# Chunked attention with a feed-forward layer: the softmax weights and the turned tokens of the later pairs by way of DRAM

## The chip, the cores and the metric

The kernel runs on one core of a Trainium2 chip. A core has five engines that run on their own and wait for each other by semaphores: TensorE (PE in the profile; its weight loads are PEld), VectorE (DVE), ScalarE (ACT), GpSimd (POOL) and SyncE (SP), which here only issues transfers. The metric is device time in microseconds (us); lower is better. A transfer (DMA) is issued by an engine's queue, here nearly always SyncE's, in program order, and is carried out by 16 DMA engines.

## The reference

Attention within chunks of 64 positions, then a normalised feed-forward layer, all in float32:

```python
scores = scale * np.matmul(q_c, k_c.transpose(0, 1, 2, 4, 3))    # (8, 8, 9, 64, 64)
scores = scores - np.max(scores, axis=-1, keepdims=True)
attn = np.exp(scores)
attn = attn / (np.sum(attn, axis=-1, keepdims=True) + 1e-09)
out = np.matmul(attn, v_c)
...
x = np.ascontiguousarray(attn_out.transpose(0, 2, 1, 3)).reshape(B, S, H * D)    # (8, 576, 512)
...
mu = np.mean(x, axis=-1, keepdims=True)
var = np.mean((x - mu) ** 2, axis=-1, keepdims=True)
xn = (x - mu) / np.sqrt(var + 1e-06) * g_ln
ch = np.maximum(xn @ w_ch1, 0.0) @ w_ch2
return (x + ch).astype(np.float32)
```

The 8 x 576 tokens are 4608 rows of 512 features; the hidden layer has 2048.

## The kernel before

**Pairs, tiles, units.** The 4608 tokens are 18 *pairs* of 256 (two blocks of 128 partitions). Two pairs are a tile, nine tiles in all. The first three tiles (pairs 0 to 5) go through a plain feed-forward (`ffn`, its products at L552 and L576) while the weights are brought in and prepared. The other six tiles are three *units* of four pairs: unit 0 is pairs 6 to 9, unit 1 is 10 to 13, unit 2 is 14 to 17. `unit_ffn` computes a unit: 28 pairs of products with seven prepared combinations of the first weights (L803, 336 products of 128x128 by 128x512), then the second weights (L888, 384 products). Its results between the two are made by ScalarE's copies (L809), VectorE's sums (L812), and the split of the hidden values into two parts (L825 on ScalarE, L830 on VectorE).

**Who runs beside whom.** `weave` interleaves the unit's products with the attention of the *next* unit's pairs: while unit 0 is computed, pairs 10 to 13 are prepared, during unit 1 pairs 14 to 17. The order is written out by hand. `attention` and `combine` are generators; `weave` counts products as it goes, and when the count reaches a position it runs the next step of the generator. Pair n of a unit begins at n * 130 + 8 (`PAIR_SPAN`, `LOADED`), and its steps come at `begin + STEPS[i]`; the loads of the pair behind it are issued with the first of them. `combine` runs 11 steps from position 345 (`FIRST_HALF`) and from 592 (`LAST_HALF`), nine apart. A unit has 720 positions. Each engine takes its instructions strictly in this order, so an instruction that waits holds all that was issued behind it on that engine, SyncE's transfers included.

**The weights' ring.** L803 and L888 read their weights from six places in SBUF that SyncE refills from DRAM (L712), one 512 KB transfer for each 12 products, each issued when the products that used the place are done.

**One pair's attention**, for the pairs at hand (neither `by_pe` nor `den_by_pe`), step by step: loads of q and k (L272); the scores, 64 small products (L300); the row maxima (L307) and the loads of v (L317); the subtraction (L332); the exponential (L335); then the softmax weights, whose rows are queries, have to be turned so that keys lie on the partitions. VectorE's transposition turns blocks of 32x32, so this takes 16 instructions of 32 partitions by 256 in four steps, each with another pair of quarters (L360, into `pt_sb`). Then the row sums and their reciprocals (L367 to L369), the outputs, 64 small products with `pt_sb` as stationary operand (L389), the scaling (L423), the statistics (L433, L434, L438, and L439 on GpSimd) and the spilling of x to DRAM (L256), the centred tokens xg on ScalarE (L452), their transposition in blocks (L478, one instruction of 128x1024, into `turned`), 16 transfers of 32 KB in four steps that put the blocks in their places in `rows` (L486, SBUF to SBUF), and the scaling with g on ScalarE (L492).

The large tiles of this chain, p_sb, pt_sb, xg and turned, share the pool `work`, which has two buffers, so a tile waits until the one that holds its buffer has been read for the last time.

**Combining.** `combine` makes the seven combinations of the turned tokens that L803 multiplies: VectorE subtracts in place (L759), and `part` splits each into a rounded part (a copy on ScalarE, L755) and the rest (a subtraction on GpSimd, L756).

**Ahead of unit 0**, the dictionary `THIRD` holds the order for the third tile's products; in it G is the attention of pair 7, which takes the same path as above, H that of pair 9, which lets TensorE turn the weights and tokens, and P and Q are `combine`.

Of the kernel before, what the change touches and what calls it, by code (L numbers as in the profile page):

```python
# [8 lines left out]
F32 = mybir.dt.float32  # L9
# [5 lines left out]
ALU = mybir.AluOpType  # L15
AX = mybir.AxisListType

P = 128
B, H, S, D = 8, 8, 576, 64
# [3 lines left out]
PAIR = 2 * P  # L23
NPAIR = T // PAIR
NTILE = NPAIR // 2
HP = H // 2
NK = DM // P
# [8 lines left out]
LEAD = 3  # L36
# [7 lines left out]
}  # L44
THIRD = {
    0: "CS", 1: "CS", 2: "DDGS", 3: "DS", 4: "DDS", 5: "DS", 6: "GS", 7: "GGHS", 8: "DG", 9: "D", 10: "GGP",
    11: "GGH", 12: "G", 13: "G", 14: "GGHP", 15: "GP", 16: "GHP", 17: "GGHP", 18: "GGHHP", 19: "HP", 20: "HHP",
    21: "HP", 22: "GPP", 23: "H", 24: "H", 26: "QQ", 27: "QR", 28: "Q", 29: "QXXN", 30: "QQR", 31: "Q",
}
ROOMS = {1: (3, 9), 2: (6,)}  # L50

PAIR_SPAN = 130
LOADED = 8
STEPS = (0, 6, 11, 16, 22, 30, 38, 46, 54, 60, 66, 72, 82, 88, 96, 106, 116, 126, 150)
ONE_STEP = 9
FIRST_HALF = 345
LAST_HALF = 592
# [36 lines left out]
def quad(i):  # L94
    return slice(32 * i, 32 * i + 32)
# [3 lines left out]
def chunk_attention_ffn(ctx: ExitStack, tc: tile.TileContext, qkv, v01, g, w, out):  # L99
    nc = tc.nc  # L100
# [4 lines left out]
    work = ctx.enter_context(tc.tile_pool(name="work", bufs=2))  # L105
    xtp = ctx.enter_context(tc.tile_pool(name="xt", bufs=2))
# [9 lines left out]
    dram = ctx.enter_context(tc.tile_pool(name="dram", bufs=1, space=bass.MemoryType.DRAM))  # L116
# [145 lines left out]

    def attention(pair, xt_cols, xs, by_pe, den_by_pe, rows_of=None, pt_raw=False):

        if pair == 1:
            qk = const.tile([P, 2, HP, PAIR], F32, name="qk_b", tag=f"w{NF - 4}")
            q_t, k_t = qk[:, 0], qk[:, 1]
        else:
            q_t = load.tile([P, HP, PAIR], F32, name="q_t")
            k_t = load.tile([P, HP, PAIR], F32, name="k_t")  # L270
# [5 lines left out]
        groups = 2 * HP  # L276
# [16 lines left out]
        s = [rows(s2[:, h2, :]) for h2 in range(2)]  # L293
        for j in range(2):
            for a in range(HP):
                for h2 in range(2):
                    r = slice(h2 * D, (h2 + 1) * D)
                    for c in range(2):
                        cs = slice(j * P + c * D, j * P + (c + 1) * D)
# [19 lines left out]
            nc.sync.dma_start(g_all, g)  # L319
        yield  # L320
        p_sb = work.tile([P, groups, 2, D], F32, name="p_sb", tag="work")
        p_b = p_sb.rearrange("p a b d -> p b a d")
        top4 = top.rearrange("p b (a one) -> p b a one", one=1).broadcast_to([P, 2, groups, D])
        if den_by_pe:
# [15 lines left out]

        if pt_raw:
            pt_sb = raws.tile([P, groups, 2, D], F32, name="pt_raw", tag="wf")
        else:
            pt_sb = work.tile([P, groups, 2, D], F32, name="pt_sb", tag="work")
        if by_pe:
            pt = halves()
            for a in range(groups):
                cs = slice(a % HP * P, (a % HP + 1) * P)
                nc.tensor.transpose(out=pt[a // HP][:, cs], in_=p_sb[:, a, :, :], identity=ident)
            for j in range(2):  # L350
                nc.scalar.copy(
                    pt_sb[:, j * HP : (j + 1) * HP], pt[j].rearrange("p (a c t) -> p a c t", a=HP, c=2)
                )
            yield
        else:
            for h2 in range(2):
                for j in range(2):
                    for c in range(2):
                        for i in range(2):
                            nc.vector.transpose(  # L360
                                out=pt_sb[quad(2 * h2 + j), :, c, quad(i)], in_=p_sb[quad(2 * c + i), :, h2, quad(j)]
                            )
                    yield
# [8 lines left out]
        if by_pe:  # L372
            o2 = banks()
            o = [o2[:, h2, :] for h2 in range(2)]
        else:
            o = [ps_h.tile([P, DM], F32, name="h") for _ in range(2)]
# [5 lines left out]
        for j in range(2):  # L382
            for a in range(HP):
                for h2 in range(2):
                    r = slice(h2 * D, (h2 + 1) * D)
                    ja = j * HP + a
                    for c in range(2):
                        cs = slice(c * D, (c + 1) * D)
# [12 lines left out]
        x = keep.tile([P, 2, DM], F32, name="x")  # L401
        if den_by_pe:
# [3 lines left out]
                out=x_j[:, 0], in0=o4[:, :, :, :D], in1=r_b[:, :, :HP].broadcast_to([P, 2, HP, D]), op=ALU.mult  # L406
            )
            for h2 in range(2):
                nc.vector.tensor_tensor(
                    out=x_j[:, 1, h2], in0=o_j[1][h2][:, :, :D], in1=r_b[:, h2, HP:].broadcast_to([P, HP, D]),  # L410
                    op=ALU.mult,
                )
            taken.remove(pair)
        elif by_pe:
            nc.vector.tensor_tensor(
                out=x.rearrange("p j (a b d) -> p b (j a) d", a=HP, b=2),
                in0=o2.rearrange("p b (a d) -> p b a d", d=D),
                in1=rden.rearrange("p a (b one) -> p b a one", one=1).broadcast_to([P, 2, groups, D]), op=ALU.mult,
            )
# [24 lines left out]
        if rows_of:  # L444
            if not by_pe:
                turned = work.tile([P, 4, 2 * NK, 32], F32, name="turned", tag="work")
            centre = small.tile([P, 2], F32, name="centre")
            nc.vector.scalar_tensor_tensor(
                out=centre, in0=mv[:, :, 0], scalar=-1.0, in1=rstd, op0=ALU.mult, op1=ALU.mult
# [5 lines left out]
        else:  # L455
            for j in range(2):
                nc.vector.scalar_tensor_tensor(
                    out=xg[:, j, :], in0=x[:, j, :], scalar=mv[:, j, 0:1], in1=g_sb, op0=ALU.subtract, op1=ALU.mult
# [1 line left out]
        yield  # L460

        if rows_of and by_pe:
            rows_t = rows_of().rearrange("p j i (k t) -> p j k i t", k=NK)
            xt = halves()
            for j in range(2):
                for k in range(NK):
                    ks = slice(k * P, (k + 1) * P)
                    nc.tensor.transpose(out=xt[j][:, ks], in_=xg[:, j, ks], identity=ident)
                for k in range(NK):
                    nc.scalar.activation(  # L470
                        rows_t[:, j, k], xt[j][:, k * P : (k + 1) * P].rearrange("p (i t) -> p i t", i=4), AF.Copy,
                        scale=g_cols[:, k : k + 1],
                    )
                yield
            return

        if rows_of:
            nc.vector.transpose(  # L478
                out=turned.rearrange("p b a t -> p a b t"),
                in_=xg.rearrange("p j (k b f) -> p (j k) b f", k=NK, b=4),  # L480
            )
            yield
            rows_t = rows_of()
            for i in range(4):
                for b in range(4):
                    nc.sync.dma_start(  # L486
                        rows_t[quad(b), :, i], turned[quad(i), b].rearrange("p (j k) t -> p j (k t)", j=2)
                    )
                yield
            for k in range(NK):  # L490
                x = rows_t.rearrange("p j i (k t) -> p (j i) k t", k=NK)[:, :, k]
                nc.scalar.activation(x, x, AF.Copy, scale=g_cols[:, k : k + 1])  # L492
            yield
            return

        xth, xtl = xt_cols()
        if by_pe:
            xt = halves()
# [21 lines left out]
        else:  # L520
            xt = work.tile([P, 2 * NK, P], F32, name="xt", tag="work")
# [214 lines left out]
    shared = {}  # L736

    def rows_of(i):
        if "rows" not in shared:
            shared["rows"] = [xtp.tile([P, 2, 2, NK, P], F32, name="rows", tag=f"xt{c}") for c in "hl"]  # L740
        return shared["rows"][i // 2][:, i % 2]

    def operand(name):
        if name not in shared:
            shared[name] = const.tile([P, 2, 2, 2 * PAIR], F32R, name="xc", tag=f"w{'2165734'.index(name)}")
        return shared[name]

    def combine(half):
        cs = slice(half * PAIR, (half + 1) * PAIR)
        a, b = (r[:, half].rearrange("p j i (k t) -> p k (j i) t", k=NK) for r in shared["rows"])  # L750
        b11, b21, b12, b22 = a[:, :2], a[:, 2:], b[:, :2], b[:, 2:]

        def part(name, x):
            o = operand(name)[:, :, :, cs].rearrange("p h k (j t) -> p h k j t", t=32)
            nc.scalar.copy(o[:, 0], x)  # L755
            nc.gpsimd.tensor_tensor(out=o[:, 1], in0=x, in1=o[:, 0].bitcast(F32), op=ALU.subtract)  # L756

        def less(out, x, y):
            nc.vector.tensor_tensor(out=out, in0=x, in1=y, op=ALU.subtract)  # L759

        part("2", b21)
        yield
        part("1", b11)
        yield
        less(b11, b12, b11)
        yield
        less(b12, b22, b12)
        yield
# [12 lines left out]
        part("4", b21)  # L781
        yield
# [205 lines left out]
    with tc.manual_schedule():  # L988
# [4 lines left out]
            G=tiles[3].attention(1), H=tiles[4].attention(1, True, pt_raw=True), S=prepare(), R=start_ring(), P=combine(0), Q=combine(1),  # L993
# [61 lines left out]
```

## Time and profile before

| | |
|---|---|
| median of 3 runs | 851.72 us (850.63 to 852.61) |
| profiled execution | 852.83 us |
| its span, first to last instruction | 851.1 us |
| TensorE's clock, mean granted | 0.999 |
| ScalarE busy | 290.0 us |
| VectorE busy | 498.1 us |
| GpSimd busy | 149.4 us |
| DMA engines, mean share by SyncE's transfers | 65.5% |

The span is what the profile covers; the execution's time lies 1.7 us above it. "Idle before, releaser" in a group's row is the time that the engine stood still just before these instructions, with what ended it. PE's idle time is what counts where TensorE is the bound; the idle time of another engine costs nothing by itself. SPq stands for SyncE's queue.

### The profile page before, as it was taken

The page shows a single profiled execution, that of the slowest core. Times are in us where ns is not written, and L with a number is a line of the kernel's source. Part 1 is how long each engine was busy: PE and PEld are TensorE (multiplying, and loading weights), DVE is VectorE, ACT ScalarE, POOL GpSimd, SP SyncE. Part 2 cuts the span into 40 slices and gives each one's busy share as a digit, 9 for nine tenths or more (in the row PEclk, how much of TensorE's full clock was granted, in tenths as well). Part 3 has the DMA queues.
Part 4 walks back from the last instruction along what each step waited for, and adds up shares of the span by engine and source line. Part 5 has one row for each costly group of instructions (what it writes and reads, how often), then busy time and mean ns, then how long its engine had stood idle before and what let it go on. Part 6 is the DMA issues. An engine that isn't in the chain of part 4 may idle for free.

```text
span 851.1 us, 14767 instructions
## 1 busy us (share of the span) xinstructions
PE 833.6 (98%) x5850; PEld 682.8 (80%) x5850; DVE 498.1 (59%) x810; ACT 290.0 (34%) x479; POOL 149.4 (18%) x138
## 2 busy tenths in 40 slices
PE   7999999999999999999999999999999999999998
PEld 4888888888888878888778888887778888888886
DVE  6989956787446536585886627658785221232321
ACT  5766431123422343234342503324534112232220
POOL 0111006474731133000220400000312200000000
PEclk9999999999999999999999999999999999999999
DMA  9997407948981237687676969777587776667572
GB/s 355 336 282 203 174 24 271 319 152 277 329 289 59 68 147 290 194 280 226 252 257 235 359 192 318 230 255 280 166 288 274 255 239 191 196 195 245 189 276 105
DMA packets 80565, 197.34 MB, mean 232 GB/s; under 512 B 8944, under 2 KB 32496, under 8 KB 78576
## 3 DMA queue, kind: packets, MB, share of 16 engines
q1 hardware_dynamic: 79200, 191.68, 65.5%
q0 software_dynamic: 1296, 4.72, 2.9%
q8 instruction: 46, 0.75, 0.4%
q14 instruction: 23, 0.19, 0.1%
HBM read 147.08 MB, written 39.85 MB: 220 GB/s over the span
## 4 chain that ended last, share of the span: by engine, by line
PE 79%; DVE 11%; DMA 3%; SPq 3%; ACT 2%; issue 1%; POOL 0%; DVEq 0%; ACTq 0%; POOLq 0%
PE y L803 22%; PE y L888 18%; PE y L576 13%; PE h L552 13%; PE h L888 8%; DVE pt_sb L360 4%; SPq L486 3%; PE s L300 2%; PE h L389 1%; DMA wp<-wfs 1%; DMA rows<-turned 1%; DMA k_t<-qkv 1%; DVE stats L433 1%; DVE hu L812 1%; PE s L389 0%
## 5 line engine op out<-in xcount | busy, mean ns | idle before, releaser
L803 PE MATMUL y<-xc,ring 128*128 128x512 f32 x1008 | 232.6, 391 | 0.0
L803 PEld LDWEIGHTS y<-xc,ring 128*128 128x128 f32 x1008 | 188.3, 188 | 39.5
L552 PE MATMUL h<-xth,wp 128*128 128x512 f32 (+1 forms) x432 | 129.5, 370 | 1.1 <-DMA wp<-wfs 1.1
L888 PE MATMUL y<-ring,hx 128*128 128x512 f32 x486 | 127.5, 390 | 1.1 <-ACT hx L825 0.8
L888 PEld LDWEIGHTS y<-ring,hx 128*128 128x128 f32 x486 | 90.9, 188 | 21.6 <-ACT hx L825 1.6
L812 DVE TENSOR_TENSOR hu<-y,snap 128x512 f32<-128x512 f32 x72 | 48.5, 683 | 91.9 <-ACT snap L809 48.0
L576 PE MATMUL y<-wp,hh 128*128 128x512 f32 x376 | 96.2, 394 | 0.0
L552 PEld LDWEIGHTS h<-xth,wp 128*128 128x128 f32 x432 | 78.2, 188 | 15.7 <-DMA wp<-wfs 1.3
L360 DVE STREAM_TRANSPOSE pt_sb<-p_sb 32x256 f32<-32x256 f32 x176 | 76.7, 436 | 11.9 <-DMA rows<-turned 6.9
L756 POOL TENSOR_TENSOR xc<-rows,xc 128x512 fp32r<-128x512 f32 x42 | 58.9, 1413 | 126.5 <-ACT xc L755 76.2
L576 PEld LDWEIGHTS y<-wp,hh 128*128 128x128 f32 x376 | 69.1, 188 | 13.9
L809 ACT COPY snap<-y 128x512 f32<-128x512 f32 x72 | 41.8, 586 | 110.0 <-PE y L803 106.7
L552 PE MATMUL h<-xtl,wp 128*128 128x512 f32 (+1 forms) x216 | 78.2, 367 | 0.0
L566 DVE SCALAR_TENSOR_TENSOR hl<-h,hh 128x512 fp32r<-128x512 f32 (+1 forms) x53 | 33.0, 629 | 72.7 <-ACT hh L565 72.4
L888 PE MATMUL y<-ring,hh 128*128 128x512 f32 x252 | 70.0, 391 | 0.0
L565 ACT ACTIVATE hh<-h 128x512 fp32r<-128x512 f32 (+1 forms) x53 | 28.5, 545 | 103.7 <-PE h L552 103.7
L830 DVE SCALAR_TENSOR_TENSOR hx<-hu,hx 128x512 fp32r<-128x512 f32 x54 | 42.8, 797 | 34.2 <-PE h L888 19.7
L888 PEld LDWEIGHTS y<-ring,hh 128*128 128x128 f32 x252 | 46.9, 188 | 10.0
L830 DVE SCALAR_TENSOR_TENSOR hl<-hu,hh 128x512 fp32r<-128x512 f32 x42 | 30.8, 737 | 39.1 <-PE h L888 16.7
L576 PE MATMUL y<-wp,hl 128*128 128x512 f32 x188 | 51.8, 389 | 0.0
L825 ACT ACTIVATE hx<-hu 128x512 fp32r<-128x512 f32 x54 | 33.3, 627 | 53.7 <-PE y L888 30.5
L888 PE MATMUL h<-ring,hx 128*128 128x512 f32 x162 | 49.9, 389 | 0.0
(132 smaller groups left out, 954.3 us busy)
## 6 DMA issues: line engine op xcount, KB each, us to landing
ring<-w2d SPq DMA_DIRECT2D x96, 512.0 KB, 4.6
ring<-wa SPq DMA_DIRECT2D x84, 512.0 KB, 4.4
raw<-w SPq DMA_DIRECT2D x15, 1024.0 KB, 7.2
out<-x SPq DMA_DIRECT2D x36, 256.0 KB, 4.7
q_t<-qkv SPq DMA_DIRECT2D x17, 512.0 KB, 5.4
k_t<-qkv SPq DMA_DIRECT2D x17, 512.0 KB, 6.5
v_t<-qkv SPq DMA_DIRECT2D x32, 256.0 KB, 6.0
w2d<-wp SPq DMA_DIRECT2D x16, 512.0 KB, 6.9
```

The costliest lines, as they stand in the source:

```text
L360: nc.vector.transpose(out=pt_sb[quad(2 * h2 + j), :, c, quad(i)], in_=p_sb[quad(2 * c + i), :, h2, quad(j)])
L552: nc.tensor.matmul(h, lhsT=(wh, wh, wl)[m][:, ks], rhs=(xth, xtl, xth)[m][:, k, :], start=i == 0, stop=i == len(terms) - 1,)
L565: nc.scalar.activation(hh, h, AF.Relu)
L566: nc.vector.scalar_tensor_tensor(out=hl, in0=h, scalar=0.0, in1=hh.bitcast(F32), op0=ALU.max, op1=ALU.subtract)
L576: nc.tensor.matmul(sums(pairs[j // 2])[j % 2], lhsT=(hh, hh, hl)[m], rhs=(wh, wl, wh)[m], start=f == 0 and m == 0, stop=f == NF - 1 and m ...
L756: nc.gpsimd.tensor_tensor(out=o[:, 1], in0=x, in1=o[:, 0].bitcast(F32), op=ALU.subtract)
L803: nc.tensor.matmul(bank, lhsT=w[:, (0, 0, 1)[m], ks], rhs=x[:, (0, 1, 0)[m], k, :], start=start and k == m == 0, stop=k == 1 and m == 2, s ...
L809: nc.scalar.copy(out, bank)
L812: nc.vector.tensor_tensor(out=out, in0=bank, in1=s, op=ALU.add)
L825: nc.scalar.activation(hh, x, AF.Relu)
L830: nc.vector.scalar_tensor_tensor(out=hl, in0=x, scalar=0.0, in1=hh.bitcast(F32), op0=ALU.max, op1=ALU.subtract)
L888: nc.tensor.matmul(ys[j], lhsT=(hh, hh, hl)[m], rhs=w[:, (0, 1, 0)[m]], start=f == 0 and m == 0, stop=f == NF - 1 and m == 2,)
```

## The change

For pairs 10 to 17 (`moved`), one transposition of the whole 128x1024 block of exponentials replaces the 16; the blocks are then put in their places by DRAM: one transfer out, and four in, one for each quarter of 32 partitions. The tile that comes back, `pt_m`, has the queries eight words apart, so the outputs' stationary operand is read with that step. For pairs 7 and 10 to 17, the turned tokens go the same way in place of the 16 transfers within SBUF. `rows` gets another layout for this, in which `part` has to be done in two halves. The steps and their positions are written anew: 16 instead of 19, and the outputs stand at 86 instead of 60. In `THIRD` pair 7 has two steps fewer, and two of pair 9's come one token later.

```diff
-    11: "GGH", 12: "G", 13: "G", 14: "GGHP", 15: "GP", 16: "GHP", 17: "GGHP", 18: "GGHHP", 19: "HP", 20: "HHP",
-    21: "HP", 22: "GPP", 23: "H", 24: "H", 26: "QQ", 27: "QR", 28: "Q", 29: "QXXN", 30: "QQR", 31: "Q",
+    11: "GGH", 12: "G", 13: "G", 14: "GGHP", 15: "GP", 16: "GHP", 17: "GHP", 18: "GHHP", 19: "HP", 20: "HHP",
+    21: "HP", 22: "GPP", 24: "H", 25: "H", 26: "QQ", 27: "QR", 28: "Q", 29: "QXXN", 30: "QQR", 31: "Q",
...
-STEPS = (0, 6, 11, 16, 22, 30, 38, 46, 54, 60, 66, 72, 82, 88, 96, 106, 116, 126, 150)
+STEPS = (0, 6, 11, 16, 22, 28, 44, 56, 86, 91, 97, 107, 113, 119, 135, 174)
...
+        moved = rows_of and not by_pe and pair >= 2 * LEAD + 4
...
+        if moved:
+            p_t = work.tile([P, 4, 32, groups], F32, name="p_t", tag="work")
...
+        if moved:
+            nc.vector.transpose(
+                out=p_t.rearrange("p b q a -> p a b q"), in_=p_sb.rearrange("p a h (j k) -> p a (h j) k", j=2)
+            )
+            yield
+            pt_there = dram.tile([P, 4, 32 * groups], F32, name="pt_there", tag=f"pt_there{pair}")
+            nc.sync.dma_start(pt_there, p_t.rearrange("p b q a -> p b (q a)"))
+            yield
+            pt_m = work.tile([P, 4, 32 * groups], F32, name="pt_m", tag="work")
+            for b in range(4):
+                nc.sync.dma_start(pt_m[quad(b)], pt_there[:, b].rearrange("(s k) x -> k s x", s=4))
+            yield
+            pt_sb = pt_m.rearrange("p (c i) (q a) -> p a c (i q)", c=2, a=groups)
...
+            there = dram.tile([P, 4, PAIR], F32, name="there", tag=f"there{pair}")
+            nc.sync.dma_start(there, turned.rearrange("p b a t -> p b (a t)"))
+            yield
             rows_t = rows_of()
-            for i in range(4):
-                for b in range(4):
-                    nc.sync.dma_start(
-                        rows_t[quad(b), :, i], turned[quad(i), b].rearrange("p (j k) t -> p j (k t)", j=2)
-                    )
-                yield
+            for b in range(4):
+                nc.sync.dma_start(rows_t[quad(b)], there[:, b].rearrange("(i f) x -> f i x", i=4))
+            yield
...
         def part(name, x):
-            o = operand(name)[:, :, :, cs].rearrange("p h k (j t) -> p h k j t", t=32)
-            nc.scalar.copy(o[:, 0], x)
-            nc.gpsimd.tensor_tensor(out=o[:, 1], in0=x, in1=o[:, 0].bitcast(F32), op=ALU.subtract)
+            for j in range(2):
+                o = operand(name)[:, :, :, cs].rearrange("p h k (j i t) -> p h j k i t", j=2, t=32)[:, :, j]
+                y = x[:, :, j::2]
+                nc.scalar.copy(o[:, 0], y)
+                nc.gpsimd.tensor_tensor(out=o[:, 1], in0=y, in1=o[:, 0].bitcast(F32), op=ALU.subtract)
```

More of the change, by code (lines that the diff above doesn't have):

```diff
@@ L342, in attention @@
             pt_sb = raws.tile([P, groups, 2, D], F32, name="pt_raw", tag="wf")
-        else:
+        elif not moved:
             pt_sb = work.tile([P, groups, 2, D], F32, name="pt_sb", tag="work")
-        if by_pe:
+        if moved:
[11 more added lines that the diff above has]
+            pt_sb = pt_m.rearrange("p (c i) (q a) -> p a c (i q)", c=2, a=groups)
+        elif by_pe:
             pt = halves()
@@ L462, in attention @@
         if rows_of and by_pe:
-            rows_t = rows_of().rearrange("p j i (k t) -> p j k i t", k=NK)
+            rows_t = rows_of().rearrange("p i (j k t) -> p j k i t", j=2, k=NK)
             xt = halves()
@@ L482, in attention @@
             yield
+            there = dram.tile([P, 4, PAIR], F32, name="there", tag=f"there{pair}")
+            nc.sync.dma_start(there, turned.rearrange("p b a t -> p b (a t)"))
+            yield
             rows_t = rows_of()
[L484 to L489 removed]
+            for b in range(4):
+                nc.sync.dma_start(rows_t[quad(b)], there[:, b].rearrange("(i f) x -> f i x", i=4))
+            yield
             for k in range(NK):
[L491 removed]
+                x = rows_t.rearrange("p i (j k t) -> p (i j) k t", j=2, k=NK)[:, :, k]
                 nc.scalar.activation(x, x, AF.Copy, scale=g_cols[:, k : k + 1])
@@ L739, in rows_of @@
         if "rows" not in shared:
-            shared["rows"] = [xtp.tile([P, 2, 2, NK, P], F32, name="rows", tag=f"xt{c}") for c in "hl"]
+            shared["rows"] = [xtp.tile([P, 2, 4, PAIR], F32, name="rows", tag=f"xt{c}") for c in "hl"]
         return shared["rows"][i // 2][:, i % 2]
@@ L749, in combine @@
         cs = slice(half * PAIR, (half + 1) * PAIR)
-        a, b = (r[:, half].rearrange("p j i (k t) -> p k (j i) t", k=NK) for r in shared["rows"])
+        a, b = (r[:, half].rearrange("p i (j k t) -> p k (i j) t", j=2, k=NK) for r in shared["rows"])
         b11, b21, b12, b22 = a[:, :2], a[:, 2:], b[:, :2], b[:, 2:]
         def part(name, x):
-            o = operand(name)[:, :, :, cs].rearrange("p h k (j t) -> p h k j t", t=32)
-            nc.scalar.copy(o[:, 0], x)
-            nc.gpsimd.tensor_tensor(out=o[:, 1], in0=x, in1=o[:, 0].bitcast(F32), op=ALU.subtract)
+            for j in range(2):
[3 more added lines that the diff above has]
+                nc.gpsimd.tensor_tensor(out=o[:, 1], in0=y, in1=o[:, 0].bitcast(F32), op=ALU.subtract)
         def less(out, x, y):
```

## The prediction

> **What bounds the kernel now.** I read the chain of work that ended last first, then the busy time by stage, then TensorE's timeline and its waits in the two stages that the change reaches. The chain's shares by line:
>
> ```profile
> PE y L803 22%; PE y L888 18%; PE y L576 13%; PE h L552 13%; PE h L888 8%; DVE pt_sb L360 4%; SPq L486 3%; PE s L300 2%; PE h L389 1%; DMA wp<-wfs 1%; DMA rows<-turned 1%; DMA k_t<-qkv 1%; DVE stats L433 1%; DVE hu L812 1%; PE s L389 0%
> ```
>
> TensorE's products fill the chain, yet two things that the change rewrites stand on the chain: the weights' transpositions (L360, 4%) and SyncE issuing the turned tokens' transfers (L486, 3%). How much of that is lost time follows from the stages. Below are unit 0, unit 1 and unit 2 (stretch, its length, then PE busy and its instructions first):
>
> ```profile
> 327.50:506.10 178.60, 175.64 (x1233) 143.25 (x1233) 115.34 (x193) 60.52 (x107) 24.61 (x19) 1.00 0.73 251
> 506.10:683.65 177.55, 175.53 (x1233) 143.21 (x1233) 114.18 (x192) 60.00 (x106) 23.71 (x18) 1.00 0.75 255
> 683.65:851.10 167.45, 163.20 (x720) 134.79 (x719) 44.25 (x65) 38.52 (x64) 0.00 (x0) 0.99 0.64 207
> ```
>
> Unit 2 has no attention beside it: 720 products in 163.20 us, 0.2267 us each, the pace at full clock (1.00, 0.99). Units 0 and 1 have the same 720 and eight groups of 64 small products (four pairs, scores and outputs). TensorE's timeline (start, length) prices one group, and shows the worst stall:
>
> ```profile
> 345.06 1.16 PE L389 MATMUL h<-v_t,pt_sb 64*64 64x64 f32 x64
> 346.15 15.26 PE L803 MATMUL y<-xc,ring 128*128 128x512 f32 x66
> 361.34 1.16 PE L300 MATMUL s<-k_t,q_t 64*64 64x64 f32 x64
> ...
> 443.77 0.33 PE L389 MATMUL h<-v_t,pt_sb 64*64 64x64 f32 x4
> 444.96 0.30 PE L389 MATMUL h<-v_t,pt_sb 64*64 64x64 f32 x2 [0.86 <-DVE pt_sb L360]
> 445.79 1.14 PE L389 MATMUL h<-v_t,pt_sb 64*64 64x64 f32 x58 [0.54 <-DVE pt_sb L360]
> 446.86 1.20 PE L888 MATMUL y<-ring,hh 128*128 128x512 f32 x4
> ```
>
> From 345.06 to 361.34 are 16.28 us; 66 products take 14.96, so an undisturbed group costs 1.32. The group at 443.77 holds TensorE for 3.09 instead of 1.09. A unit without stalls would take 163.20 + 8 x 1.32 = 173.76 us: unit 0 loses 4.84, unit 1 loses 3.79, together **8.63 us**. That is all that the change can win in them. TensorE's waits there, unit 0, then unit 1 (total, times, longest):
>
> ```profile
> PE h L389 <- DVE pt_sb L360: 2.3, 4, 0.9
> PE y L888 <- ACT hx L825: 0.4, 1, 0.4
> PE y L888 <- DVE hx L830: 0.3, 1, 0.3
> ```
> ```profile
> PE h L389 <- DVE pt_sb L360: 1.6, 3, 0.7
> PE y L888 <- ACT hx L825: 0.4, 1, 0.4
> ```
>
> Idle is 3.9 us at the output groups and 1.1 at L888; the 8.63 (idle, and each restart of the pipeline) I divide likewise: **6.7 us at L389**, 1.9 at L888. Why L389 waits shows on VectorE and on SyncE's queue ahead of the stall at 443.77:
>
> ```profile
> 436.82 3.58 DVE L360 STREAM_TRANSPOSE pt_sb<-p_sb 32x256 f32<-32x256 f32 x8 [2.54 <-DMA rows<-turned]
> 440.43 0.95 DVE L830 SCALAR_TENSOR_TENSOR hx<-hu,hx 128x512 fp32r<-128x512 f32 x1
> 441.42 1.79 DVE L360 STREAM_TRANSPOSE pt_sb<-p_sb 32x256 f32<-32x256 f32 x4
> 443.22 0.69 DVE L830 SCALAR_TENSOR_TENSOR hl<-hu,hh 128x512 fp32r<-128x512 f32 x1
> 443.92 1.81 DVE L360 STREAM_TRANSPOSE pt_sb<-p_sb 32x256 f32<-32x256 f32 x4
> ```
> ```profile
> 432.48 2.50 SPq L486 DMA_DIRECT2D rows<-turned  x4
> 435.08 0.53 SPq L712 DMA_DIRECT2D ring<-w2d  x1
> 435.71 0.38 SPq L272 DMA_DIRECT2D q_t<-qkv  x1
> ```
>
> The pool `work` has two buffers; pt_sb's is the one that the previous pair's `turned` leaves, so VectorE stands 2.54 us until the last of 16 small transfers has landed, then needs 7.2 us for 16 transpositions, and the outputs stand behind them.
>
> **The change, part by part.**
>
> ```profile
> L360 DVE STREAM_TRANSPOSE pt_sb<-p_sb 32x256 f32<-32x256 f32 x176 | 76.7, 436 | 11.9 <-DMA rows<-turned 6.9 <-ACT p_sb L335 2.4
> ...
> L478 DVE STREAM_TRANSPOSE turned<-xg 128x1024 f32<-128x1024 f32 x9 | 11.2, 1244 | 10.6 <-ACT xg L452 10.6
> ```
>
> *Transpositions.* 16 x 0.436 = 7.0 us become one of 128x1024, as L478: 1.24. The new one writes with a step of 32 bytes, which no row shows; bounds 1.24 and twice that, 2.5. I take 1.24, and the other 1.2 would only come off the slack worked out below, since the outputs stand 64 positions behind it. VectorE loses 8 x 5.8 = 46 us of work in the two units and, when `turned` leaves by one transfer, the wait for its buffer (6.9 in all). What L389 waited for on VectorE is gone: **-6.7 us**.
>
> *The trip through DRAM.* What is late next is this. Count from the start T of a pair's scores; positions are products of 0.2267 us.
>
> ```profile
> 394.73 1.16 PE L300 MATMUL s<-k_t,q_t 64*64 64x64 f32 x64
> ```
> ```profile
> 400.11 1.06 ACT L335 ACTIVATE p_sb<-p_sb 128x1024 f32<-128x1024 f32 x1 [0.60 <-DVE p_sb L332]
> ```
>
> The exponentials end at T + 6.4, the transposition at T + 7.7; SyncE comes to position 28 at 1.32 + 6.35 = T + 7.7. The nearest rows for the transfers are the spilled tokens (512 KB out to DRAM), the values (256 KB in) and L486 on SyncE (issue, then size and landing):
>
> ```profile
> DMA to landing us min/median/max: 2.7/3.4/6.5
> ```
> ```profile
> DMA to landing us min/median/max: 3.0/6.0/13.2
> ```
> ```profile
> L486 SPq DMA_DIRECT2D rows<-turned x144: 585/594/1669, 282.2 to 643.7; - x144
> ```
> ```profile
> rows<-turned SPq DMA_DIRECT2D x144, 32.0 KB, 2.2
> ```
>
> Out: landed at T + 11.1 (14.2 at worst); SyncE stands at position 44, T + 11.3, by then. Four transfers in at 0.59 each: issued by T + 13.7, landed by T + 15.9 if they land as L486's do (2.2), by T + 19.7 at the values' 6.0. The outputs stand at 1.32 + 86 x 0.2267 = **T + 20.8**. Slack is 1.1 to 4.9 us at medians, and at the worst of all rows (14.2 + 2.4 + 13.2 = 29.8) the outputs are 9.0 late. I take nothing, near the medians. While SyncE waits, the ring's fetches stand behind it, for up to 3 us here; six places, each used for 12 products (2.7 us), leave a fetch five uses, 13.6 us, to land, so nobody waits for that.
>
> *The outputs' weight loads.* They now read every eighth word.
>
> ```profile
> L389 PEld LDWEIGHTS h<-v_t,pt_sb x704: 129/135/135, 151.1 to 624.2; 64*64 64x64 f32 x176
> L389 PE MATMUL h<-v_t,pt_sb x704: 218/218/267, 151.1 to 624.3; 64*64 64x64 f32 x176
> ```
>
> All these loads read neighbouring words; no row has a load with a step. Below nothing is excluded, the count stays. At the other end, a load at half pace: the group's 1.16 us less the last product's 0.22 is 0.94 of starts, in which loads and products run side by side; doubled, each pair's outputs cost 0.94 more, 8 x 0.94 = 7.5 us. I take nothing, by the nearest row, and keep 7.5 for the range.
>
> *The turned tokens.* 16 issues of 0.59 become five. From the transfers in (position 135) to the scaling (174) are 39 positions, 8.8 us, against 2.4 + 6.0 at the values' median: hidden by products. If it isn't, ScalarE stands at the scaling with L809's copies behind it; `combine` only follows at 345, when the first two pairs have been done since 312. For pair 7, ahead of unit 0, I count nothing: bounds are 1 us either way, about TensorE's one wait there.
>
> *The split of `part`.* 14 copies and 14 subtractions per call of `combine` for 7 and 7, half as wide.
>
> ```profile
> L756 POOL TENSOR_TENSOR xc<-rows,xc 128x512 fp32r<-128x512 f32 x42 | 58.9, 1413 | 126.5 <-ACT xc L755 76.2 <-DMA ring<-w2d 38.6 <-PE y L888 7.6
> ...
> L492 ACT ACTIVATE rows<-rows,g_sb 128x256 f32<-128x256 f32 x36 | 15.3, 497 | 19.3 <-DMA rows<-turned 19.3
> ```
>
> A half-wide copy is 0.50 at most by L492, so a part is at most 1.0 on ScalarE; on GpSimd between 1.41 and 2.8 for two. A part has nine positions, 2.0 us, and GpSimd is idle beside it. But L888 waits for ScalarE, which gets more work: I leave all 1.9 us of L888's stalls.
>
> **The sum.** -6.7 + 0. The profiled execution took 852.83 (span 851.1, 1.7 around it): 846.1. It is 1.1 above the median of the runs, 851.72, so the median comes to **845.0**, 0.8% faster.
>
> **The rivals.**
>
> *1, the loads pay for their step (same time).* For it: loads and products of a group fill the 0.94 us side by side with nothing to hide a slower load. Against: nothing but the missing row. 846.1 + 7.5, as a median 852.5.
>
> [...]
>
> *2, the trip is late (slower).* In the fourth pair of a unit, the brought-back tokens and the next pair's loads share the transfers, and they are full:
>
> ```profile
> 444.00:446.00 2.00, 0.61 (x18) 0.40 (x18) 1.91 (x5) 0.00 (x0) 0.00 (x0) 1.00 1.03 422
> ```
>
> (share 1.03 of 16 engines, 422 GB/s). Half of the 9.0 us of lateness in that pair of both units is 9.0: 855.1, as a median 854.0. It ends slower than before once the eight pairs are late by 6.7 us together. Against: without the 16 issues SyncE, which now issues the next pair's loads (435.71) only after the last of the 16, can send them ahead of the trip.
>
> *3, loads at a third of the pace:* 15 us, a median of 860.
>
> *4, the change does not do what it says:* VectorE's L812 and L830, not the transpositions, hold the outputs, and the stall moves with them: half is won, 848.4.
>
> **Chances.** Forecast 0.50 (its own range 842.5 to 848: the low end takes L888's stalls too, 843.1, and pair 7), rival 1 0.24, rival 2 0.14, rival 3 0.06, rival 4 0.06. The range 842.5 to 856 leaves out rival 3, the worse half of rival 2 and a little below, under 0.2. A measurement of this kernel can tell about 0.2% (1.7 us) from no change. Faster by more: 0.50 + 0.04 of rival 4 + 0.02 of rival 1 = 0.56; same: 0.14 of rival 1 + 0.02 of rival 4 = 0.16; slower 0.28.
>
> **What would show it.** Right: no wait of L389 in units 0 and 1, both stages near 175 us, no wait of L360's successor for a buffer. Rival 1: the outputs' group over 1.16 us with no wait before it. Rival 2: L389 waiting for pt_m's transfers. Rival 4: L389 waiting for p_t. The forecast is wrong if either the group grows or a transfer ends its wait.

## The result, and the profile after

The changed kernel takes **860.89 us** (median of 4 runs, 858.79 to 861.38) against 851.50 for the kernel before beside it (4 runs): ratio 1.0105, 95% interval 1.0084 to 1.0126, slower. The forecast was 845.0, with a range up to 856. The profiled execution took 861.13 us, its span 859.4, 8.3 longer than before.

The page's chain by line, of the changed kernel:

```profile
PE y L821 24%; PE y L906 17%; PE y L592 15%; PE h L568 14%; PE h L906 8%; DMA pt_there<-p_t 3%; PE h L405 2%; PE s L301 2%; DMA rows<-there 2%; DMA pt_m<-pt_there 2%; DMA wp<-wfs 1%; DMA k_t<-qkv 1%; PE s L405 1%; SPq L358 1%; DMA ring<-w2d 0%
```

The transpositions (4%) and SyncE's issuing of the turned tokens (3%) have left the chain; the trip through DRAM is on it in their place: 3% out, 2% in, 1% issuing. (L821 and L906 are the old L803 and L888, L405 the outputs, L349 the new transposition, L354 and L358 the trip out and in, L500 and L504 the tokens' way out and in, L728 the ring.) The three units of the changed kernel, by windows (stretch, length, PE busy and its instructions first; clock, DMA share and GB/s last), and TensorE's waits in the first two of them (total, times, longest):

```profile
326.29:511.81 185.52, 179.74 (x1233) 148.16 (x1232) 91.90 (x133) 62.48 (x122) 29.46 (x34) 0.99 0.84 276
511.81:692.04 180.23, 178.65 (x1233) 147.48 (x1232) 91.91 (x132) 61.79 (x120) 27.95 (x32) 1.00 0.86 286
692.04:859.40 167.36, 163.36 (x721) 134.95 (x719) 44.25 (x65) 38.53 (x64) 0.00 (x0) 1.00 0.64 207
```
```profile
PE h L405 <- DMA pt_m<-pt_there: 7.4, 7, 3.0
```

All waits of before are gone, on VectorE at the outputs and on ScalarE and VectorE at the second weights. One kind is left, and it is new. But PE is also *busy* longer with the same 1233 instructions. The outputs' rows say why (weight loads, then products; min/median/max ns), and TensorE's timeline shows a group that waited for nothing:

```profile
L405 PEld LDWEIGHTS h<-v_t,pt_m x512: 191/213/219, 349.5 to 638.1; 64*64 64x64 f32 x171
L405 PE MATMUL h<-v_t,pt_m x512: 280/280/379, 349.5 to 638.2; 64*64 64x64 f32 x171
```
```profile
349.46 2.16 PE L405 MATMUL h<-v_t,pt_m 64*64 64x64 f32 x64
```

A load takes 213 ns where it took 135, a product 280 where it took 218, a group 2.16 us where it took 1.16, now that the loads read with a step of 32 bytes. The first two runs below separate the step from the trip.

The sum closes with three terms. A stall-free unit was 173.76 us; with four groups 1.00 longer it is 177.76. The units of the changed kernel are 7.76 and 2.47 above that. So: +8.0 for the loads' step, +10.2 for the late trip (7.4 of idle, the rest restarts and a lower clock, below), -8.6 for the old stalls; unit 0 began 1.2 sooner and unit 2 was 0.1 shorter. That is +8.3.

Where the lateness comes from shows on SyncE's queue ahead of the fourth pair of unit 0 and on TensorE behind it (start, length; the wait ahead in brackets):

```profile
431.03 0.33 SPq L273 DMA_DIRECT2D q_t<-qkv  x1
431.41 0.42 SPq L273 DMA_DIRECT2D k_t<-qkv  x1
432.10 1.82 SPq L504 DMA_DIRECT2D rows<-there  x4
433.97 1.48 SPq L318 DMA_DIRECT2D v_t<-qkv  x2
435.55 3.72 SPq L728 DMA_DIRECT2D ring<-w2d  x2
439.69 1.01 SPq L260 DMA_DIRECT2D x<-x_d  x2
440.92 0.32 SPq L354 DMA_DIRECT2D pt_there<-p_t  x1
441.48 0.32 SPq L728 DMA_DIRECT2D ring<-w2d  x1
449.83 1.74 SPq L358 DMA_DIRECT2D pt_m<-pt_there  x4
```
```profile
453.24 0.46 PE L405 MATMUL h<-v_t,pt_m 64*64 64x64 f32 x4 [3.01 <-DMA pt_m<-pt_there]
455.57 2.20 PE L405 MATMUL h<-v_t,pt_m 64*64 64x64 f32 x60 [1.87 <-DMA pt_m<-pt_there]
```

In ten microseconds SyncE issues the next pair's q and k, the previous pair's tokens, v, two pieces of the ring and the two pieces of x that unit 0's last sums add (`x<-x_d`), eight times 512 KB, and only then the transfer out; its landing, which the transfers in wait for, comes 8.8 us later. Landings of the three kinds (columns: size, median us):

```profile
rows<-there SPq DMA_DIRECT2D x36, 128.0 KB, 6.4
pt_there<-p_t SPq DMA_DIRECT2D x8, 512.0 KB, 6.9
pt_m<-pt_there SPq DMA_DIRECT2D x32, 128.0 KB, 3.3
```

And the one transposition took 2.14 us in place of 1.24, writing with the same step of 32 bytes that the loads read with:

```profile
L349 DVE STREAM_TRANSPOSE p_t<-p_sb x8: 2126/2142/2216, 335.1 to 619.7; 128x1024 f32<-128x1024 f32 x8
```

### The profile page after: what moved, and what is told of

Its sections match the earlier page's. It is cut to its first block, busy times and chain, and to the rows that moved or that the text cites. A ratio compares the mean times of both kernels' runs of the same rounds, so it can differ in the third digit from the quotient of the medians.

```text
span 859.4 us, 14685 instructions
## 1 busy us (share of the span) xinstructions
PE 841.5 (98%) x5850; PEld 692.7 (81%) x5850; DVE 451.4 (53%) x690; ACT 295.3 (34%) x521; POOL 161.3 (19%) x180
## 4 chain that ended last, share of the span: by engine, by line
PE 85%; DMA 9%; DVE 3%; SPq 1%; issue 1%; ACT 0%; DVEq 0%
PE y L821 24%; PE y L906 17%; PE y L592 15%; PE h L568 14%; PE h L906 8%; DMA pt_there<-p_t 3%; PE h L405 2%; PE s L301 2%; DMA rows<-there 2%; DMA pt_m<-pt_there 2%; DMA wp<-wfs 1%; DMA k_t<-qkv 1%; PE s L405 1%; SPq L358 1%; DMA ring<-w2d 0%
## 5 line engine op out<-in xcount | busy, mean ns | idle before, releaser
L821 PE MATMUL y<-xc,ring 128*128 128x512 f32 x1008 | 231.9, 390 | 0.0
L821 PEld LDWEIGHTS y<-xc,ring 128*128 128x128 f32 x1008 | 188.4, 188 | 39.5
L906 PE MATMUL y<-ring,hx 128*128 128x512 f32 x486 | 127.3, 391 | 0.0
L906 PEld LDWEIGHTS y<-ring,hx 128*128 128x128 f32 x486 | 91.4, 189 | 19.2
L774 POOL TENSOR_TENSOR xc<-rows,xc 128x256 fp32r<-128x256 f32 x84 | 70.1, 863 | 141.0 <-ACT xc L773 122.6
L906 PE MATMUL y<-ring,hh 128*128 128x512 f32 x252 | 69.4, 390 | 0.0
L848 DVE SCALAR_TENSOR_TENSOR hx<-hu,hx 128x512 fp32r<-128x512 f32 x54 | 39.4, 735 | 51.3 <-ACT hx L843 23.5
L906 PEld LDWEIGHTS y<-ring,hh 128*128 128x128 f32 x252 | 47.1, 188 | 9.8
L906 PE MATMUL h<-ring,hx 128*128 128x512 f32 x162 | 49.9, 389 | 0.0
L455 POOL TENSOR_TENSOR rstd<-vare,mhalf 128x2 f32<-128x2 f32 x12 | 9.5, 794 | 214.3 <-DVE vare L454 214.3
```

What stands on the lines that cost most here:

```text
L774: nc.gpsimd.tensor_tensor(out=o[:, 1], in0=y, in1=o[:, 0].bitcast(F32), op=ALU.subtract)
L821: nc.tensor.matmul(bank, lhsT=w[:, (0, 0, 1)[m], ks], rhs=x[:, (0, 1, 0)[m], k, :], start=start and k == m == 0, stop=k == 1 and m == 2, s ...
L848: nc.vector.scalar_tensor_tensor(out=hl, in0=x, scalar=0.0, in1=hh.bitcast(F32), op0=ALU.max, op1=ALU.subtract)
L906: nc.tensor.matmul(ys[j], lhsT=(hh, hh, hl)[m], rhs=w[:, (0, 1, 0)[m]], start=f == 0 and m == 0, stop=f == NF - 1 and m == 2,)
```

## The experiments

Two costs were to be told apart: the step of the outputs' loads, and a trip that comes late. For the second, a further question was whether the transfers are slow or only stand behind others. Each ratio is to the kernel before, run beside the kernel in question (its medians were 851.5 to 852.5 us); "below the changed kernel" is the difference of the median from 860.89. Waits and stages are those of one traced execution.

**The step taken away.** The stationary operand reads neighbouring words of `pt_m`; the trip stays.

```diff
-            pt_sb = pt_m.rearrange("p (c i) (q a) -> p a c (i q)", c=2, a=groups)
+            pt_sb = pt_m.rearrange("p b x -> p (b x)").rearrange("p (a c q) -> p a c q", a=groups, c=2)
```

> The changed kernel, but the outputs' stationary operand is read word by neighbouring word from pt_m instead of every eighth word (the softmax weights then stand in another order; every transfer, wait and count stays). Theory A, the step of the loads costs time: the group of 64 output products goes from 2.16 us back to 1.16, eight groups give 8.0 us, the time comes to about 853. Rival, the groups are long because the transfers of the trip hold up TensorE's reading: groups stay at 2.16, time 861.

Measured: 852.71 us (10 runs, 849.62 to 862.34), ratio 1.0009 (0.998 to 1.0039): 8.2 below the changed kernel. The loads:

```profile
L405 PEld LDWEIGHTS h<-v_t,pt_m x512: 129/135/228, 348.8 to 637.8; 64*64 64x64 f32 x171
L405 PE MATMUL h<-v_t,pt_m x512: 218/218/363, 348.8 to 637.8; 64*64 64x64 f32 x171
```

They are back at 135 and 218 ns with the trip in place, so the step alone makes them slow. The profiled execution is the highest of the ten (862.34), so its stages are not used. Its waits for the trip are 12.5 us where the changed kernel's trace has 7.4 with the same trip, so a single trace gives the idle time only to within some microseconds. The waits for the trip remain, which the next two runs leave out.

**The step alone, in the kernel before.** From pair 10 on the outputs read `pt_sb` with the step; nothing goes through DRAM.

```diff
+        if rows_of and not by_pe and pair >= 2 * LEAD + 4:
+            pt_sb = pt_sb.rearrange("p a c q -> p (a c q)").rearrange("p (c q a) -> p a c q", c=2, a=groups)
```

> The kernel before, with nothing changed but that the outputs of pairs 10 to 17 read their stationary operand every eighth word (the softmax weights then stand in another order). Theory A: each of the eight groups grows by 1.0 us, the time from 851.5 to about 859.5. Rival, it is the extra transfers: groups stay at 1.16 us where no wait falls into them, time 851.5.

Measured: 857.15 (10 runs), ratio 1.0053 (1.0038 to 1.0068), 4.9 above the kernel before. In the profiled execution (860.25) the units last 182.87 and 181.46 by windows, 4.3 and 3.9 above those of before, and this is left of TensorE's waits:

```profile
PE h L391 <- DVE pt_sb L360: 3.6, 4, 1.6
```

The groups grow by 1.00 in the kernel before too, and the two units of this execution by 8.2. The medians differ by less, 4.9, where 8.0 was expected: the profiled execution is the highest of its ten. The waits of 1.1 at the second weights are gone here, but whether the other executions gave back the rest in stalls isn't shown.

**No trip.** The outputs read `p_t` itself with the step, the blocks stay where the transposition left them, and the five transfers are gone.

```diff
-            nc.sync.dma_start(pt_there, p_t.rearrange("p b q a -> p b (q a)"))
...
-                nc.sync.dma_start(pt_m[quad(b)], pt_there[:, b].rearrange("(s k) x -> k s x", s=4))
...
-            pt_sb = pt_m.rearrange("p (c i) (q a) -> p a c (i q)", c=2, a=groups)
+            pt_sb = p_t.rearrange("p (c i) q a -> p a c (i q)", c=2)
```

> The changed kernel without the trip of the softmax weights through DRAM: the outputs read p_t as the transposition leaves it (with the same step; the blocks are not put in their places). Theory B, the trip is late and the outputs wait for it: the 7.4 us of idle at the outputs go, and with the restarts some 10 us; groups stay at 2.16, time about 851. Rival, VectorE's transposition or something else ahead of the trip is late: the wait moves to p_t, time 858 or more.

Measured: 849.38 (10 runs), ratio 0.9964 (0.995 to 0.9977), 11.5 below the changed kernel. TensorE waits for nothing in units 0 and 1; groups are 2.16, and the units last 177.73 and 177.74 us, against the 173.76 + 4 x 1.00 = 177.76 of the sum above. So of the changed kernel's two units, 10 us are the late trip and 8 the step.

**The tokens' half of the change alone.** `moved` is false: the weights are turned by 16 instructions, only the turned tokens go through DRAM. Steps at the old positions up to 96, then 112 and 150.

```diff
-        moved = rows_of and not by_pe and pair >= 2 * LEAD + 4
+        moved = False
```

> Only the turned tokens go through DRAM; the softmax weights keep the 16 transpositions of before, with the positions of before as far as the outputs. If the buffer that turned holds was what made the transpositions late, VectorE no longer waits at the first of them (6.9 us before), and of the 6.7 us of stalls at the outputs over half goes: about 846. Rival, the 16 transpositions (7.2 us) are late by themselves: about 850.

Measured: **843.58** (4 runs, 843.08 to 844.28), ratio 0.9888 (0.9861 to 0.9914), the fastest of all here. Its units by windows, its wait at the outputs, and VectorE at the place of the 2.54 us wait shown in the prediction:

```profile
324.49:499.22 174.73, 174.34 (x1234) 142.68 (x1233) 110.98 (x193) 61.92 (x122) 29.32 (x34) 1.00 0.79 269
499.22:673.99 174.77, 174.38 (x1233) 142.68 (x1232) 110.53 (x192) 61.43 (x120) 27.87 (x32) 1.00 0.80 271
```
```profile
PE h L405 <- DVE pt_sb L376: 0.8, 2, 0.4
```
```profile
429.99 3.58 DVE L376 STREAM_TRANSPOSE pt_sb<-p_sb 32x256 f32<-32x256 f32 x8
```

The transposition finds its buffer free, since `turned` leaves by one transfer. VectorE works as long as before on the weights, and still the outputs hardly wait. The two units are 6.65 us shorter than before, of the 8.63 that the stalls cost: most of the stalls came from the 16 transfers, and at most 2.0 us from the 16 transpositions. Unit 0 also begins 3.0 us sooner here. The other kernels with the changed order ahead of unit 0 begin it 0.9 to 2.7 sooner, so how much of that belongs to the change isn't settled.

**The weights' half alone.** The tokens by 16 transfers as before, at 119, 127, 135 and 143 of the new steps.

```diff
-STEPS = (0, 6, 11, 16, 22, 28, 44, 56, 86, 91, 97, 107, 113, 119, 135, 174)
+STEPS = (0, 6, 11, 16, 22, 28, 44, 56, 86, 91, 97, 107, 113, 119, 127, 135, 143, 174)
```

> Only the softmax weights go through DRAM; the turned tokens keep their 16 transfers within SBUF, in four steps of four. Theory: both costs sit in the weights' part, and the 16 issues stand on SyncE's queue ahead of the next trip: idle at the outputs as in the changed kernel or worse, 861 to 865. Rival, the tokens' trip is what delays the weights' trip: idle under 3 us, about 854.

Measured: 900.99 (4 runs), ratio 1.0575 (1.0556 to 1.0593), far outside both expectations. VectorE's largest waits and one of its transpositions in unit 0 show that another thing was measured:

```profile
DVE p_t L349 <- DMA rows<-turned: 39.3, 4, 10.7
```
```profile
376.44 2.03 DVE L349 STREAM_TRANSPOSE p_t<-p_sb 128x1024 f32<-128x1024 f32 x1 [9.14 <-DMA rows<-turned]
```

So late, the 16 transfers hold `turned` until after the next pair's transposition is due in the same buffer; VectorE stands with the units' sums behind it. It is the old stall of 2.54 us grown to 9 to 11. As a measure of the weights' half by itself the run is of no use; that half is known only through the other runs.

**What stands ahead of the trip: the next pair's loads.** They are issued at position 62 of the pair, behind the trip.

```diff
-                    side.append((begin + STEPS[0], following(u + 1, n + 1)))
+                    side.append((begin + 62, following(u + 1, n + 1)))
```

> The changed kernel with the next pair's loads of q and k issued 62 positions after the scores, behind the trip, and no longer with them. Theory B', the transfer out (6.9 us to landing, against 3.5 for the same size of turned tokens) stands behind these loads: it lands in about 4 us, the 7.4 us of idle at the outputs go, groups stay at 2.16; about 851. Rival, the trip is slow by itself (transposition 2.14, out, in): idle stays over 5 us, about 860.

Measured: 855.76 (9 runs), ratio 1.0039 (1.0024 to 1.0054), 5.1 below the changed kernel.

```profile
PE h L405 <- DMA pt_m<-pt_there: 2.5, 4, 1.1
```

Idle falls from 7.4 to 2.5, all of it in the fourth pairs. From the issue of the transfer out to that of the transfers in ("out to in"), by pairs, are 3.0, 7.9, 6.3, 9.0 and 3.2, 7.9, 5.6, 9.7 us; the transfer out itself lands in 2.9, 6.3, 6.2, 8.9 and 3.2, 5.0, 4.7, 9.6. Only the first pair of a unit, which has no previous pair's tokens ahead of it, has a free way. The time lies between the two expectations: by it, the loads were half of the matter.

**Also the tokens behind the trip.** The loads at 62 stay. In the first three pairs of a unit the tokens' transfers in and their scaling now come after the next pair's trip.

```diff
-FIRST_HALF = 345
+AFTER_NEXT = STEPS[:-2] + (186, 225)
+FIRST_HALF = 364
...
-                    side += [(begin + at, following(u + 1, n)) for at in STEPS]
+                    side += [(begin + at, following(u + 1, n)) for at in (AFTER_NEXT if n < 3 else STEPS)]
```

> The changed kernel with what stood ahead of the trip on SyncE's queue taken away: the next pair's loads of q and k are issued after this pair's trip (position 62), and for the first three pairs of a unit the turned tokens' transfers in come after the next pair's trip (186 in place of 135, the scaling at 225 in place of 174, the first half of combine at 364 in place of 345). Theory Q (the trip is late only for what stands ahead of it in the queue): the transfers in of every pair are issued some 3 us after the transfer out (first pairs of b3 showed 3.0 and 3.2; the changed kernel 4.5 to 8.9), TensorE's idle time at the outputs falls from 2.5 us (b3) to below 0.7, units 0 and 1 last 177.7 us each as without any trip, and the time is 849 to 851. Theory T (the trip itself is slow: its small rows or its transposed pattern): out to in stays above 5 us for the second to fourth pairs, idle at the outputs stays near 2.5 us, the time is 855 to 857. Group of outputs 2.16 us with either.

Measured: 850.92 (10 runs), ratio 0.9984 (0.9974 to 0.9995), 10.0 below the changed kernel. Units and wait (outputs at L406 here):

```profile
325.53:503.80 178.27, 178.19 (x1234) 147.08 (x1232) 93.81 (x133) 62.43 (x122) 29.46 (x34) 1.00 0.86 287
503.80:682.36 178.56, 178.18 (x1234) 147.07 (x1232) 93.38 (x132) 61.82 (x120) 28.50 (x32) 1.00 0.87 289
```
```profile
PE h L406 <- DMA pt_m<-pt_there: 0.4, 1, 0.4
```

The units are within 0.9 us of those without any trip: the same five transfers, with the same pattern, at the same positions, cost 1.4 us in both units together when less is issued ahead of them. One number missed: out to in is 3.0 to 3.7 us in the first two pairs of a unit, but stays at 5.6 to 7.4 in the third and fourth. SyncE's waits at the transfers in (L359 here) show two different things:

```profile
SPq L359 <- DMA pt_there<-p_t: 17.8, 6, 6.4
...
SPq L359 <- DVE den L384: 6.9, 2, 4.6
```

In the third pairs the transfer out lands in 2.8 and 3.2 us, and the wait that ends last is for VectorE's row sums (L384): the transfers in are issued 0.07 us after these are done, in both units. In the fourth pairs the landing itself takes 7.2 and 6.7, behind the 1 MB of x that SyncE fetches some 2 us earlier. So the transfer out is fast (2.8 to 3.6 us) in the six pairs that have a free way, and the outputs, 58 positions behind it, hide the rest.

**The trip on GpSimd's queue.** The same positions, another issuer.

```diff
-            nc.sync.dma_start(pt_there, p_t.rearrange("p b q a -> p b (q a)"))
+            nc.gpsimd.dma_start(pt_there, p_t.rearrange("p b q a -> p b (q a)"))
```

(and the same for the four in).

> The changed kernel with the five transfers of the weights' trip issued by GpSimd in place of SyncE, at the same positions. Theory Q (what stands ahead in SyncE's queue makes the trip late): out to in falls below 5 us where GpSimd is free, idle at the outputs below 3 us, 852 to 856. Rival (GpSimd is no freer: its subtractions wait for ScalarE and for buffers, and the transfers stand behind them; or its issuing takes longer): idle at the outputs stays at 7 us or more, 859 to 866.

Measured: 890.88 (4 runs), ratio 1.046 (1.0406 to 1.0513), worse than the rival's case.

```profile
PE h L405 <- DMA pt_m<-pt_there: 18.3, 12, 3.9
```
```profile
380.02 2.21 POOL L358 DMA_DIRECT2D pt_m<-pt_there  x4 [7.77 <-PE y L821]
```

GpSimd stands 7.77 us at an issue that the trace puts down to a product of TensorE. But the transfers in read what the transfer out writes, and SyncE's queue stood at the same place for its landing in the changed kernel (40.2 us, seven times), so I take it that they wait for this landing here too. In the next pair 7.9 us pass from the issue of the transfer out (411.73) to that of the transfers in (419.64), though none of SyncE's transfers stands ahead of it on this queue, and all eight groups of outputs wait: 25.4 us in all, of which the trace puts 18.3 down to `pt_m`. So leaving SyncE's queue doesn't free the trip. Whether it is late because the DMA engines carry SyncE's transfers at the same time, or because transfers issued by GpSimd are slower by themselves, this run can't tell.

**The quarters in another order.** In the changed kernel, share and rate stand oddly to each other while quarter transfers are in flight (windows of 2 us, DMA share and GB/s last): a full share moves 219 and 208 GB/s in the first and the last, and 387 in the one between, with whole tiles in flight.

```profile
436.00:438.00 2.00, 2.00 (x10) 1.67 (x9) 2.00 (x2) 1.82 (x6) 1.56 (x3) 1.00 1.14 219
440.00:442.00 2.00, 2.00 (x11) 1.65 (x10) 0.00 (x0) 0.43 (x2) 0.19 (x1) 1.00 1.02 387
...
452.00:454.00 2.00, 0.46 (x4) 0.35 (x4) 0.00 (x0) 0.00 (x0) 0.00 (x0) 1.00 1.10 208
```

```diff
-            for b in range(4):
+            for b in (0, 2, 1, 3):
```

(for the weights' four and for the tokens').

> The changed kernel with the four transfers in (of the weights and of the turned tokens) issued in the order first, third, second, fourth quarter of the partitions; nothing else is changed. In the changed kernel, while quarter transfers are in flight, the 16 DMA engines show a full share (1.02 to 1.14) but move only 200 to 230 GB/s, about half of what they move for whole tiles (368 to 406 GB/s). [...] Theory R (the rate is that of one transfer of 32 partitions with rows of 1 KB, whatever goes beside it): rate and landings stay within 0.3 us and the time within 859 to 862.

Measured: 857.78 (4 runs), ratio 1.0077 (1.0056 to 1.0098), 3.1 below the changed kernel by medians, though the two intervals overlap.

```profile
rows<-there SPq DMA_DIRECT2D x36, 128.0 KB, 5.3
...
pt_m<-pt_there SPq DMA_DIRECT2D x32, 128.0 KB, 2.9
```
```profile
434.00:436.00 2.00, 2.00 (x11) 1.65 (x10) 2.00 (x2) 1.52 (x5) 1.86 (x3) 1.00 1.13 240
...
448.00:450.00 2.00, 0.00 (x0) 0.00 (x0) 0.00 (x0) 0.00 (x0) 0.00 (x0) 1.00 1.01 276
```

The tokens land in 5.3 in place of 6.4, the weights in 2.9 in place of 3.3, at 240 and 276 GB/s in place of 219 and 208; idle at the outputs is 4.1 in place of 7.4, a difference between single traces. Both landings moved by more than theory R's 0.3 us, by 1.1 and 0.4, and the time lies below its 859 to 862: the order of the four matters here. The rates are shown; that the 3.1 us come from them is likely, not shown. Why the order of the four changes their rate no run shows.

**Both costs taken away.** The run with the tokens later, and neighbouring words for the loads.

> The same as the run with the tokens' transfers later, and besides the outputs' stationary operand is read word by neighbouring word (the weights of a block come in another order, so the outputs are not the reference's). If the changed kernel's loss has just two parts, the step of the loads and the lateness of the trip, both are gone: group 1.16 us, loads 135 ns, products 218 ns, units 0 and 1 near 173.8 to 174.5 us, time 841 to 843.5, as low as the kernel that sends only the tokens through DRAM (843.6). If there is a third part (transposition 0.9 us longer, the split in halves, another order ahead of unit 0), it stays above 845.

Measured: 844.98 (4 runs, 842.86 to 847.87), ratio 0.9917 (0.9889 to 0.9945): 15.9 below the changed kernel, against 8.2 and 10.0 for each alone. Unit 0 lasts 174.49; unit 1 lasts 179.44 in this execution, the highest of the four, and its only wait is this:

```profile
PE y L907 <- ACT hh L844: 3.8, 3, 2.4
```

The median lies just above the expected 841 to 843.5 and below the 845 of a third part. In this execution, the slowest of the four, what is left is a wait at the second weights for ScalarE's split of the hidden values; the other three have no trace. The weights' half, freed of both costs, doesn't beat the tokens' half alone.

**Halves in place of a step.** A stationary operand of neighbouring words, but 128 products of 32 columns for 64 of 64 (the block's order in `p_t` is changed to match).

```diff
+                            for i in range(2):
+                                nc.tensor.matmul(
+                                    rows(o[h2])[quad(2 * c + i), ja, :], lhsT=pt_sb[r, ja, c, i],
+                                    rhs=v_t[j][r, a, c, :], start=True, stop=True,
+                                )
```

> The changed kernel with the weights brought back so that 32 queries lie word by word, and each output product cut in two of 32 columns, which read them so: no step in the loads, none in the transposition's writes, 128 products for 64 in a group. Theory A (the step costs): groups go back towards 1.2 us, the transposition to 1.24 us, the trip ends 0.9 us sooner; about 852. Rival, the number of products sets the pace of a group: groups stay near 2 us, about 860.

Measured: 865.26 (4 runs), ratio 1.0151 (1.0124 to 1.0178), although the transposition, which now writes neighbouring words of the same `p_t`, is back at 1.24 us, and a group without a wait is 0.67 shorter than with the step:

```profile
348.55 1.49 PE L406 MATMUL h<-v_t,pt_m 64*32 64x64 f32 x128
```
```profile
PE h L406 <- DMA pt_m<-pt_there: 8.3, 5, 2.8
PE h L406 <- issue: 4.1, 1, 4.1
PE y L828 <- issue: 1.4, 1, 1.4
```

The trip is as late as before, and TensorE stands 5.5 us for nothing that the profile shows. What that is remains open.

**The tokens' half with later outputs.** The 0.8 us that the outputs still wait in the best version were to go by six positions more.

```diff
-STEPS = (0, 6, 11, 16, 22, 30, 38, 46, 54, 60, 66, 72, 82, 88, 96, 112, 150)
+STEPS = (0, 6, 11, 16, 22, 30, 38, 46, 54, 66, 72, 78, 88, 94, 102, 118, 154)
```

> Only the turned tokens through DRAM, with the outputs and all behind them six positions later than in the run with the tokens alone. The last two stalls at the outputs (0.39 us each and a restart of 0.3) go: about 842.2. Rival, the later steps run into the split of the hidden values and cost as much: 843.6 or more.

Measured: 845.31 (4 runs), ratio 0.992 (0.9904 to 0.9937), not faster. The wait moved:

```profile
PE y L821 <- DVE hu L830: 2.7, 2, 1.4
```

## Why the prediction was wrong

- **"What L389 waited for on VectorE is gone: -6.7 us"** held, and more: the 1.9 us at L888 went as well, 8.6 in all. But the change's two halves were credited together. The tokens' half alone takes 6.65 of the 8.63 us out of the two units (843.58): it was mostly the buffer held by 16 transfers that made VectorE late, and the 46 us of work taken off VectorE were worth the other 2.0 at most.
- **"The outputs' weight loads ... I take nothing, by the nearest row"** failed. The nearest rows all read neighbouring words, so they couldn't speak on the step. The bound from the other side was nearly exact: 0.94 a group and 7.5 in all, measured 1.00 and 8.0. Rival 1 was right in mechanism and size.
- **"The trip through DRAM ... I take nothing, near the medians"** failed. The 3.4 us is the median of all 14 transfers of spilled tokens: the six ahead of unit 0 have 3.0, the eight within units 0 and 1 have 4.5, so the row of the right stage was slower already. This one lands in 6.9; in the worst pair 4 MB were issued in the ten microseconds ahead of it; the transposition took 0.9 more (within its bounds). Out issued at T + 8.2 to 11.1, in at T + 12.6 to 20.0, and four of the eight groups of outputs, due at T + 20.8, waited, seven times in all. The worst case worked out there was 9.0 late; the worst group stood 4.9 us (3.01 and 1.87).
- **The argument against rival 2** had its sign turned. That SyncE sends the next pair's loads sooner was to speak for the trip; those loads were about half of what it waited behind, as moving them showed (5.1 us of the 10.2).
- **Rivals 1 and 2 were taken as alternatives**, each with a time near the one before. They concern different engines and add: +8.0 and +10.2. Had they been combined, the case 845.0 + 7.5 + 9.0 = 861.5 would have stood in the list; the range ended at 856. That this is so near 860.89 is luck in part: both costs were 1.7 larger together, and the stalls gave 1.9 more. Rival 3's 860 was met by accident: the loads went at half the pace (1.00 a group), not at a third.
- What stood: the ring's fetches behind a waiting SyncE hurt nobody (no wait of TensorE for the ring, though the queue stood up to 7.9 us at L358); the turned tokens' longer way is hidden; the split of `part` costs GpSimd 2 x 0.86 us for 1.41, within its bounds, and TensorE never waits for it. Ahead of unit 0 nothing was counted, with bounds of 1 us; the changed kernel's trace begins unit 0 1.2 sooner, which the spread between the kernels above leaves open.

## What to carry to other kernels

Before a transfer is given the landing time of its like, list what its queue and the DMA engines hold at that moment: the same 512 KB out took 3.3 us or 6.9 (medians) by what SyncE had issued ahead of it, and on GpSimd's queue 7.9 passed before the transfers in were issued. A layout that saves instructions on one side can be paid for on the other, as this one was where it is read and written with a step (a load 213 ns for 135, a transposition 2.14 us for 1.24), so price the reader too, and take the bound as the forecast when every nearest row lacks the very property in question. Rivals that act on different engines are added, not weighed against each other; and where a change has two halves, ask which of them the removed wait belongs to.

## What the runs showed of the hardware that was not expected

- The step of 32 bytes cost on the writing side too: VectorE's 128x1024 transposition takes 2.14 us into `p_t` with the step and 1.24 into the same tile without it (the run with halves).
- After the longest stall of the changed kernel the granted clock of TensorE fell. Behind the 4.9 us of idle at 450 to 455.6 in the changed kernel, three windows (clock, share and rate last) and the timeline's next products:

```profile
454.00:456.00 2.00, 0.43 (x14) 0.46 (x16) 0.00 (x0) 0.00 (x0) 0.00 (x0) 0.84 0.95 342
456.00:458.00 2.00, 2.00 (x57) 1.89 (x53) 0.40 (x1) 0.00 (x0) 0.00 (x0) 0.50 1.04 406
458.00:460.00 2.00, 2.00 (x8) 1.59 (x8) 1.93 (x5) 0.00 (x0) 0.00 (x0) 0.81 0.58 234
```
```profile
457.70 5.99 PE L906 MATMUL y<-ring,hx 128*128 128x512 f32 x23
```

  The clock is 0.84, 0.50 and 0.81, and 23 products take 5.99 us where 23 x 0.2267 are 5.21. In the kernel before, with stalls of under 1 us, both units had 1.00. In the run with both costs taken away, 15 products behind a wait of 2.35 us (from 628.73 to 633.88) take 5.15 us where 15 x 0.2267 are 3.40, while four products behind a wait of 0.97 us take 1.19, as four behind an undisturbed group of outputs do. So these two longer waits cost more than their length: 0.8 of the 2.8 us by which the lateness exceeds the idle time are here.
- The order in which four quarters of a tile are fetched changes their rate (from 208 to 276 GB/s in the windows shown).
